# Query masks built by GpSimd block copies, and half of an output-projection block loaded by eight transfers of every eighth partition

## The chip, the cores and the metric

The kernel runs on one core of one Trainium2 chip. The metric is the device time of one execution in microseconds; the profiled span is about 2 us shorter than it. Three runs of the kernel before took 1343.92 to 1344.07 us, median 1344.0. "Fast" here means within 1.5% of the fastest run of the same kernel.

## The reference, cut to what matters

One decode step of attention over a cached K and V, with a small gated MLP beside it. Attention moves nearly all the bytes: K and V are 256 MB each, `wq` and `wo` 8 MB each, in bf16.

```python
B, Sq, D = 4, 1, 1024
H, Sk, Dh = 32, 8192, 128
q = (x @ wq).reshape(B, Sq, H, Dh).transpose(0, 2, 1, 3)
scores = jnp.einsum("bhqd,bhkd->bhqk", q, k_cache) * (Dh ** -0.5)
p = softmax(scores)
o = jnp.einsum("bhqk,bhkd->bhqd", p, v_cache)
a = o.transpose(0, 2, 1, 3).reshape(B, Sq, H * Dh) @ wo
out = g * a + (1 - g) * b          # b: a one-token MLP; g: a sigmoid gate
```

Every byte of K, V and the weights is used once, so the kernel can be no faster than its loads.

## The kernel before

All large loads are issued by SyncEngine (`nc.sync`) in program order. They land in a ring of five 4 MB slots. K is transposed by DVE and multiplied with a masked query `Z` on PE; V is multiplied with the softmax weights on PE.

```python
ring = const.tile([P, NS, RING], BF, name="ring")      # NS = 5 slots, 4 MB each

def load_pair(src, n, apart=False):                     # one pair: 4 heads, 8 MB
    a = slots(2)
    if a + 1 < NS and not apart:
        nc.sync.dma_start(out=flat[:, lo:lo + 2 * n], in_=src)
        ...
    for i, half in enumerate(halves):                   # two halves of 4 MB
        nc.sync.dma_start(out=half[:, 0:n], in_=src[:, i * n:(i + 1) * n])

def wo_block(g, r0=0, r1=FR):                           # 1 MB of wo: 512 rows
    w = wo_home[home][:, at]
    nc.sync.dma_start(out=w[:, r0:r1]..., in_=wov[:, g, r0:r1]...)
    def use():
        ... mm_acc(acc[...], LT[:, r, g, :], w[:, r, ...])
    return use

def spread(d):                                          # the masked query Z
    nc.vector.tensor_tensor(out=Z[...], in0=qa[:, :, h0:h0 + NQ, b],
                            in1=mq[:].to_broadcast([P, 4, NQ]), op=ALU.mult)
```

The last V pair comes in six pieces (two of 2 MB and four of 1 MB), so that PE can follow closely. The end of the program is:

```python
    # in v_pair, for the last pair d == ND - 1
    for half, cuts in ((0, 2), (1, 4)):
        for c in range(cuts):
            nc.sync.dma_start(out=vs[half][:, lo:hi], in_=vv[...])
...
for kind, d in order:
    ...
    if (kind, d) == ("v", ND - 1):
        for g in range(2):
            wo_block(g)()          # wo blocks 0 and 1, ahead of the last V pair
    if kind == "v":
        v_pair(d)
...                                # then wo blocks 2 to 7
```

The scheduler gives each transfer a completion semaphore, from eight in rotation (the trace's issues carry eight numbers, 101 to 105 and 108 to 110, in turn). A transfer therefore may not be issued before the one eight places ahead of it in the queue has landed; I call this the rule of eight. In the trace of the kernel before, the last landing of the V half is at 1298.95 us, and the last V piece, eight places behind it, is issued at 1299.01. The compiled SyncEngine stream of the kernel before shows it at the tail (`DMAHW` are the rotating semaphores; earlier transfers carry no such wait because a wait on PE already implies it):

```
L196 V 128x16384      [waits PE]           x3     halves of the last-but-one pairs
L388 wo 128x4096      [waits PE]           x2     wo blocks 0 and 1
L515 V 128x8192       [waits PE]           x2     last V pair, 2 MB pieces
L515 V 128x4096       [waits PE]           x2     last V pair, 1 MB pieces
L515 V 128x4096       [waits DMAHW3, PE]
L515 V 128x4096       [waits DMAHW4, PE]
```

(The lines are shortened.) I call the last 4 MB transfer of the last-but-one V pair "the V half".

Of the kernel before, what the change touches and what calls it, by code (L numbers as in the profile page):

```python
# [8 lines left out]
BF = mybir.dt.bfloat16  # L9
F32 = mybir.dt.float32  # L10
U32 = mybir.dt.uint32
# [101 lines left out]
def kernel(  # L113
# [61 lines left out]
    def turned(rows, n, dtype=BF):  # L175
        t = TB[tb_turn[0] % 3]
        tb_turn[0] += 1
        return t[0:rows, 0:n] if dtype == BF else t[0:rows, 0:2 * n].bitcast(dtype)

    def slots(n):  # L180
        at = turn[0]
        turn[0] = (at + n) % NS
        return at
# [15 lines left out]
    def small(shape, dtype=F32):  # L199
        return mps.tile(shape, dtype, name="small", tag="small")  # L200
# [15 lines left out]
        nc.vector.memset(z[:], 0.0)  # L216
    acc = acc4[0:Bn].rearrange("p z n -> p (z n)")

    row = const.tile([P, P], F32)
    nc.vector.memset(row[:, 0:1], 0.0)  # L220
    n = 1
    while n < P:
        nc.vector.tensor_scalar(out=row[:, n:2 * n], in0=row[:, 0:n], scalar1=float(n), scalar2=None, op0=ALU.add)
        n *= 2
    col = const.tile([P, 32], F32)
    nc.vector.transpose(out=col[:].bitcast(U32), in_=row[:, 0:32].bitcast(U32))
    for n in range(32, P, 32):
        nc.vector.tensor_scalar(out=col[n:n + 32], in0=col[n:n + 32], scalar1=float(n), scalar2=None, op0=ALU.add)
    ident = const.tile([P, P], F32)
    nc.vector.tensor_scalar(out=ident[:], in0=row[:], scalar1=col[:, 0:1], scalar2=None, op0=ALU.is_equal)  # L230
    identb = const.tile([P, P], BF)
    nc.vector.tensor_copy(out=identb[:], in_=ident[:])
    xw_ps = small([P, DT, NX], BF)
# [5 lines left out]
    R = ptp.tile([P, 4, P], BF, name="R", tag="PTs")  # L239
    for half in range(2):  # L240
        for e in range(2):
            turns = ident[:, 64 * half + e:64 * half + 64:2]
            for n in range(4):
                nc.vector.tensor_copy(out=R[:, 2 * half + e, 32 * n:32 * n + 32], in_=turns)

    mask3 = const.tile([P, GD, NQ], F32)
    nc.vector.tensor_reduce(out=mask3[:], in_=ident[:].rearrange("p (q t r) -> p t q r", q=NQ, t=GD), axis=AX.X, op=ALU.add)
# [2 lines left out]
    one = ident[:].rearrange("p (t e s a) -> p e a t s", t=GD, e=2, s=NQ)  # L250
    for a in range(4):
        nc.vector.tensor_tensor(out=selg[:, a], in0=one[:, 0, a], in1=one[:, 1, a], op=ALU.add)
    mE4 = const.tile([P, 2, 4], F32)
    nc.vector.tensor_reduce(out=mE4[:], in_=ident[:].rearrange("p (n e r) -> p e n r", n=4, e=2), axis=AX.X, op=ALU.add)
    mE = const.tile([P, 2], F32)
    nc.vector.tensor_reduce(out=mE[:], in_=mE4[:], axis=AX.X, op=ALU.add)
    mq4 = const.tile([P, NQ], F32)
    nc.vector.tensor_reduce(out=mq4[:], in_=ident[:].rearrange("p (q r) -> p q r", q=NQ), axis=AX.X, op=ALU.add)
    mq = const.tile([P, 1, NQ], BF)
    nc.vector.tensor_copy(out=mq[:, 0, :], in_=mq4[:])  # L260
    ones = const.tile([P, P], F32)
    nc.gpsimd.memset(ones[:], 1.0)
    mx, mxT, ng, ngT = [const.tile([P, 32], F32, name=f"mx{i}") for i in range(4)]
    nc.vector.memset(mx[:], 0.0)
    ZW = QP - 1 + P + 1
    Zt = [const.tile([P, 4, ZW], BF, name=f"Z{i}") for i in range(2)]
    PB = const.tile([P, QP, 2, 2, 2, NQ, 4], BF, name="PB")
# [5 lines left out]
    qa = const.tile([P, 4, H, Bn], BF)  # L273
    OT = const.tile([P, H, Bn], BF)
    LT = const.tile([P, FR, H // FR, Bn], BF)
    hT = const.tile([P, FG, FR, Bn], BF)
    sgb = const.tile([P, 2, Bn], F32)
    c12 = const.tile([P, 2, Bn], F32)
# [91 lines left out]
    def o_rows(g0, g1):  # L370

        n = g1 - g0
        lp = small([P, FR, n, Bn])
        for k in range(WB):
            for r in range(FR):
                nc.tensor.matmul(lp[32 * k:32 * k + 32, r], lhsT=identb[:, r:P:FR],  # L376
                                 rhs=OT[:, WB * g0 + k:WB * g1:WB, :], start=True, stop=True, skip_group_check=True)
        nc.vector.tensor_copy(out=LT[:, :, g0:g1, :], in_=lp[:])  # L378

    wo_home = {}  # L380

    def wo_block(g, r0=0, r1=FR):

# [40 lines left out]
    def spread(d):  # L424
        b, h0 = heads(d)
        Z = Zt[d % 2]
        nc.vector.tensor_tensor(out=Z[:, :, QP - 1:QP - 1 + P].rearrange("p e (q c) -> p e q c", c=QP)[:, :, :, 0],  # L427
                                in0=qa[:, :, h0:h0 + NQ, b], in1=mq[:].to_broadcast([P, 4, NQ]), op=ALU.mult)

    def k_pair(d):  # L430
        g, t = divmod(d, GD)
# [29 lines left out]
    def softmax(g):  # L461
        sps = S_ps.pop(g)

        nc.vector.tensor_reduce(out=mx[:, 0:1], in_=sps[:].rearrange("p z n -> p (z n)"), axis=AX.X, op=ALU.max)  # L464
        nc.vector.transpose(out=mxT[:].bitcast(U32), in_=mx[:].bitcast(U32))
        gm = stat.tile([P, GD], F32, tag="gm")
        nc.vector.tensor_reduce(out=gm[:], in_=mxT[:].rearrange("p (t r) -> p t r", r=RD), axis=AX.X, op=ALU.max)
        nc.vector.tensor_scalar(out=ng[:].rearrange("p (t r) -> p t r", r=RD), in0=gm[:].unsqueeze(2).to_broadcast([P, GD, RD]),
                                scalar1=-scale, scalar2=None, op0=ALU.mult)
        nc.vector.transpose(out=ngT[:].bitcast(U32), in_=ng[:].bitcast(U32))  # L470
        negm = ngT
        PTs = ptp.tile([P, 1024], BF, name="PTs", tag="PTs")
        rs = stat.tile([P, 1], F32, tag="rs")
        nc.scalar.activation(out=PTs[:], in_=sps[:].rearrange("p z n -> p (z n)"), func=ACT.Exp, bias=negm[:, 0:1], scale=scale, accum_out=rs[:, 0:1])  # L474
        PT = ptp.tile([P, 32, 32], BF, name="PT")
        nc.vector.transpose(out=PT[:].rearrange("p j i -> p (j i)"), in_=PTs[:])  # L476
        rex = stat.tile([P, GH], F32, tag="rex")
        nc.vector.tensor_scalar(out=rex[:], in0=mask, scalar1=rs[:, 0:1], scalar2=None, op0=ALU.mult)

        def inverse():  # L480
            tot = small([P, GH])
            nc.tensor.matmul(tot[:, :], lhsT=ones[:], rhs=rex[:], start=True, stop=True)  # L482
            rinv = stat.tile([P, GH], F32, name="rinv", tag="rinv")
            nc.vector.reciprocal(out=rinv[:], in_=tot[:, :])  # L484
            rinv_t[g] = rinv
        late.append(inverse)

        def spread_p():
            Pv = PT[:].rearrange("p (q j) i -> p i q j", j=4)
            Bv = PB[:].rearrange("p i z w e s j -> p i (z w e) s j")  # L490
            for q in range(NQ):
                at = slice(QP * q, QP * (q + 1))
                if q % 2 == 0:
                    nc.scalar.copy(out=Bv[at, :, :, q, :], in_=Pv[at])  # L494
                else:
                    nc.gpsimd.tensor_copy(out=Bv[at, :, :, q, :], in_=Pv[at])  # L496
        behind.append(spread_p)
# [66 lines left out]
    for kind, d in order:  # L564
        if kind == "k":
            k_pair(d)
            if d in side:
                side[d]()
        if (kind, d) == ("v", ND - 1):
            for g in range(2):  # L570
                wo_block(g)()
        if kind == "v":
            v_pair(d)
        if (kind, d) == ("k", ND // 2):
            add_x()
        if (kind, d) == ("v", ND - 2):
            o_rows(0, GE)
# [45 lines left out]
```

## Time and profile before

| | before |
|---|---|
| time, median | 1344.0 us |
| DMA: share of 16 engines' span in the main queue | 99.5% |
| mean rate | 429 GB/s |
| PE, DVE, POOL busy | 77%, 46%, 3% |
| V half landed (PE's wait for it ended) | 1298.99 us |
| PE's last wait for wo ended | 1337.33 us |

These are lines of the profile's page of the kernel before: the span, the busy times, two rows of 40 slices (busy tenths of the DMA engines, GB/s), two queues (packets, MB, share) and the shares of the chain that ended last.

```profile
span 1342.0 us, 7617 instructions
...
PE 1037.2 (77%) x4552; PEld 228.1 (17%) x2364; DVE 621.8 (46%) x434; ACT 50.6 (4%) x46; POOL 35.5 (3%) x24
...
DMA  9999999999999999999999999999999999999997
...
q1 hardware_dynamic: 14276, 575.69, 99.5%
q8 instruction: 27, 0.44, 0.1%
...
DMA 69%; DVE 19%; PE 11%; issue 0%; ACT 0%; SPq 0%; DVEq 0%
```

The DMA engines are full in every slice but the last. No compute engine bounds the kernel, and the chain's DVE and PE parts only free ring slots while earlier loads are still queued. So a change can gain only by filling the DMA engines at the end, and can lose by letting them run dry. The line of queue 8 is 27 packets of 16 KB that fetch instructions.

Next is SyncEngine's timeline of the kernel before, around the tail (start, length, engine, line, operation, transfer, count; a group that waits inside is long):

```profile
1270.38 0.33 SPq L196 DMA_DIRECT2D ring<-in_A_v_cache_dram  x1
1272.11 2.05 SPq L388 DMA_DIRECT2D ring<-in_A_wo_dram  x2
1279.68 19.66 SPq L515 DMA_DIRECT2D ring<-in_A_v_cache_dram  x6
1301.43 7.74 SPq L388 DMA_DIRECT2D ring<-in_A_wo_dram  x3
```

The first line is the issue of the V half. wo blocks 0 and 1 follow at once, and the last V pair from 1279.68, almost 20 us before the V half has landed. That is the queue's lead. And these are windows of the kernel before (window in us, its length and the busy times of PE, PEld, DVE, ACT and POOL, then the granted clock, the DMA share, GB/s):

```profile
1280.00:1290.00 10.00, 10.00 (x51) 2.33 (x25) 0.00 (x0) 0.00 (x0) 0.00 (x0) 1.00 1.02 439
1292.00:1302.00 10.00, 7.31 (x28) 1.50 (x14) 0.00 (x0) 0.00 (x0) 0.00 (x0) 0.83 0.99 415
1302.00:1312.00 10.00, 9.68 (x66) 2.58 (x40) 0.23 (x1) 0.00 (x0) 0.00 (x0) 1.00 1.00 423
```

One more fact comes from the trace's packet records, which carry no engine's number; I joined packets that follow one another without a gap into 16 strings. Towards the end seven strings run ahead of the other nine: their last bytes of wo land at 1331.7 to 1332.5, the others' at 1336.0 to 1338.2. All 16 together would be level at about (7 x 1332 + 9 x 1337) / 16 = 1335, so evening them out could gain some 3 us at most (an estimate from these times).

### The profile page before, as it was taken

Reading aid. Unit: us, or ns where it says so; the run is one execution under the profiler, and the core shown is the slowest. Engines: PE = TensorE matmul, PEld = TensorE weight load, DVE = VectorE, ACT = ScalarE, POOL = GpSimd, SP = SyncE. Lnnn points to the kernel's source line nnn. Section 1 sums busy time; section 2 is a strip of 40 time slices with the busy share of each in tenths; the row PEclk is TensorE's granted clock in tenths of the full one; section 3 lists DMA queues with packets and bytes.
Section 4 is the critical chain, followed back from the end, with each engine's and each line's share of the span. In section 5 each row is a group of like instructions: output and inputs, shape, how many; then the busy total and the mean of one; then the engine's idle time right before and its main releaser. Section 6 shows DMA issues by size and latency. Waiting matters only on the chain.

```text
span 1342.0 us, 7617 instructions
## 1 busy us (share of the span) xinstructions
PE 1037.2 (77%) x4552; PEld 228.1 (17%) x2364; DVE 621.8 (46%) x434; ACT 50.6 (4%) x46; POOL 35.5 (3%) x24
## 2 busy tenths in 40 slices
PE   2565878787788687778987779597778678877898
PEld 0111111111111121111211112111111112111222
DVE  3555655545346554336455556046555254556000
ACT  0000100001000010001000010000100010000100
POOL 1000100001000010001000010000100010000100
PEclk9777988988998888899988889898889799888999
DMA  9999999999999999999999999999999999999997
GB/s 416 437 432 430 436 436 427 447 428 421 441 426 429 443 436 423 437 434 430 438 434 430 432 427 436 436 432 438 428 425 433 432 433 440 436 419 446 419 424 327
DMA packets 14316, 576.18 MB, mean 429 GB/s; under 512 B 1598, under 2 KB 1606, under 8 KB 2252
## 3 DMA queue, kind: packets, MB, share of 16 engines
q1 hardware_dynamic: 14276, 575.69, 99.5%
q8 instruction: 27, 0.44, 0.1%
q14 instruction: 5, 0.04, 0.0%
q10 hardware_dynamic: 8, 0.00, 0.0%
HBM read 575.68 MB, written 0.01 MB: 429 GB/s over the span
## 4 chain that ended last, share of the span: by engine, by line
DMA 69%; DVE 19%; PE 11%; issue 0%; ACT 0%; SPq 0%; DVEq 0%
DMA ring<-in_A_k_cache_dram 58%; DVE TB L443 19%; DMA ring<-in_A_v_cache_dram 7%; PE o_ps L523 7%; PE S_ps L449 3%; DMA ring<-in_B_w_gate_dram 3%; DMA ring<-in_A_wo_dram 1%; PE o_ps L315 0%; DVE Z L427 0%; PE acc L315 0%; PE acc L281 0%; PE small L482 0%; PE small L543 0%; DVE OS L536 0%; ACT OS L535 0%
## 5 line engine op out<-in xcount | busy, mean ns | idle before, releaser
L443 DVE STREAM_TRANSPOSE TB<-ring 128x2048 uint32<-128x2048 uint32 x256 | 569.4, 2280 | 487.7 <-DMA ring<-in_A_k_cache_dram 485.6
L449 PE MATMUL S_ps<-TB,Z 128*128 128x512 bf16 x2048 | 522.8, 411 | 216.5 <-DVE TB L443 216.0
L523 PE MATMUL o_ps<-ring,PB 128*32 128x512 bf16 x2048 | 461.3, 387 | 52.5 <-DMA ring<-in_A_v_cache_dram 48.0
L449 PEld LDWEIGHTS <-Z 128*128 128x128 bf16 x1024 | 106.1, 104 | 628.4 <-issue 626.8
L523 PEld LDWEIGHTS <-PB 128*32 128x32 bf16 x1024 | 100.5, 98 | 404.9 <-issue 394.9
L496 POOL COPY PB<-PT 32x1024 bf16<-32x1024 bf16 x16 | 30.5, 1905 | 1223.9 <-PE o_ps L523 1069.8
L474 ACT ACTIVATE PTs<-S_ps,mx 128x1024 bf16<-128x1024 f32 x8 | 8.9, 1114 | 1019.7 <-DVE mx L470 1019.7
L536 DVE SCALAR_TENSOR_TENSOR OS<-o_ps,mE,OS 128x512 f32<-128x512 f32 x8 | 6.0, 751 | 70.8 <-ACT OS L535 70.8
L494 ACT COPY PB<-PT 32x1024 bf16<-32x1024 bf16 x16 | 30.6, 1910 | 1.6 <-DVE PT L476 1.4
L484 DVE RECIPROCAL rinv<-small 128x16 f32<-128x16 f32 x8 | 2.1, 258 | 41.5 <-PE small L482 41.5
L378 DVE CAST LT<-small 128x64 bf16<-128x64 f32 x2 | 0.5, 225 | 44.0 <-PE small L376 44.0
L235 PE MATMUL small<-identb,x 6*128 6x6 bf16 x8 | 0.6, 197 | 22.2 <-DMA x<-in_A_x_dram 22.2
L464 DVE TENSOR_REDUCE mx<-S_ps 128x1 f32<-128x1024 f32 x8 | 9.8, 1225 | 15.9 <-PE S_ps L449 15.9
L281 PE MATMUL acc<-ring,LT 128*4 128x512 bf16 x64 | 14.8, 379 | 1.7 <-DMA ring<-in_A_wo_dram 0.9
L476 DVE STREAM_TRANSPOSE PT<-PTs 128x1024 bf16<-128x1024 bf16 x8 | 10.0, 1245 | 10.2 <-ACT PTs L474 10.2
L281 PE MATMUL acc<-ring,hT 128*4 128x512 bf16 x56 | 12.2, 379 | 0.0
L535 ACT ACTIVATE OS<-o_ps,mE 128x512 f32<-128x512 f32 x8 | 5.5, 687 | 163.4 <-PE o_ps L523 163.4
L543 PEld LDWEIGHTS small<-selg,OS 128*128 128x128 f32 x64 | 8.4, 195 | 4.1 <-issue 3.9
L315 PE MATMUL o_ps<-ring,xw 128*4 128x512 bf16 x56 | 5.3, 505 | 3.9 <-DMA ring<-in_B_w_gate_dram 3.9
L543 PE MATMUL small<-selg,OS 128*128 128x16 f32 x64 | 8.1, 259 | 0.0
L237 DVE COPY xw<-small 128x48 bf16<-128x48 bf16 x1 | 0.2, 182 | 14.9 <-PE small L235 14.9
L315 PE MATMUL S_ps<-ring,xw 128*4 128x512 bf16 x64 | 6.3, 582 | 0.3 <-DVE xw L237 0.3
(68 smaller groups left out, 72.6 us busy)
## 6 DMA issues: line engine op xcount, KB each, us to landing
ring<-in_A_k_cache_dram SPq DMA_DIRECT2D x14, 4096.0 KB, 34.2
ring<-in_A_v_cache_dram SPq DMA_DIRECT2D x14, 4096.0 KB, 31.3
ring<-in_B_w_gate_dram SPq DMA_DIRECT2D x1, 7168.0 KB, 37.2
ring<-in_B_w_up_dram SPq DMA_DIRECT2D x1, 7168.0 KB, 39.2
ring<-in_B_w_down_dram SPq DMA_DIRECT2D x2, 3584.0 KB, 27.3
ring<-in_A_wo_dram SPq DMA_DIRECT2D x6, 1024.0 KB, 24.7
ring<-in_A_v_cache_dram SPq DMA_DIRECT2D x2, 2048.0 KB, 30.5
ring<-in_A_v_cache_dram SPq DMA_DIRECT2D x4, 1024.0 KB, 24.6
```

What stands on the lines that cost most here:

```text
L281: nc.tensor.matmul(out_ap, lhsT=lhsT, rhs=rhs, start=start, stop=True, skip_group_check=True)
L315: nc.tensor.matmul(ps[32 * k:32 * k + Bn, z, :], lhsT=xT[TW * half + t], rhs=cols(w, t, 4 * z + k), start=(half + t == 0), stop=(half == 1 ...
L443: nc.vector.transpose(out=flat_t.bitcast(U32), in_=kn[:, c * CJ * Dh:(c + 1) * CJ * Dh].bitcast(U32))
L449: nc.tensor.matmul(sps[:, z, :], lhsT=Z[:, he, s:s + P], rhs=T[:, 16 * z:16 * z + 16, half, :, e], start=(t == 0 and n == 0 and he == 0), ...
L464: nc.vector.tensor_reduce(out=mx[:, 0:1], in_=sps[:].rearrange("p z n -> p (z n)"), axis=AX.X, op=ALU.max)
L474: nc.scalar.activation(out=PTs[:], in_=sps[:].rearrange("p z n -> p (z n)"), func=ACT.Exp, bias=negm[:, 0:1], scale=scale, accum_out=rs[:, ...
L476: nc.vector.transpose(out=PT[:].rearrange("p j i -> p (j i)"), in_=PTs[:])
L494: nc.scalar.copy(out=Bv[at, :, :, q, :], in_=Pv[at])
L496: nc.gpsimd.tensor_copy(out=Bv[at, :, :, q, :], in_=Pv[at])
L523: nc.tensor.matmul(o_ps[row:row + NM, e, :], lhsT=PB[:, RD * t + c, z, w].rearrange("p e s j -> p (e s j)"), rhs=vn[:, j0 * Dh:(j0 + 4) * ...
L536: nc.vector.scalar_tensor_tensor(out=o_sb[:], in0=o_ps[:, 1, :], scalar=mE[:, 1:2], in1=o_sb[:], op0=ALU.mult, op1=ALU.add)
L543: nc.tensor.matmul(oT[:, :], lhsT=o_sb[:, q * Dh:(q + 1) * Dh], rhs=selg[:, q].rearrange("p t s -> p (t s)"), start=(q == 0), stop=(q == 3))
```

## The change

The intent is twofold. First, DVE is relieved: masks and the masked queries `Z` are built by GpSimd copies, block by block, instead of DVE products. Second, half of wo's first block is loaded in a way that is meant to give some DMA engines more bytes than others. Rows 0 to 255 of wo go onto partitions 0 to 63, in eight transfers of eight partitions each; rows 256 to 511 come in a normal 128-partition transfer.

```diff
@@ spread(d): the masked query
-        nc.vector.tensor_tensor(out=Z[...][:, :, :, 0],
-                                in0=qa[:, :, h0:h0 + NQ, b], in1=mq[:].to_broadcast([P, 4, NQ]), op=ALU.mult)
+        for q in range(NQ):
+            at = slice(QP * q, QP * (q + 1))
+            nc.gpsimd.tensor_copy(out=Z[at, :, QP - 1 + QP * q], in_=qa[at, :, h0 + q, b])
@@ new
+    def wo_first():
+        wo_home[0] = ring[:, slots(1)].rearrange("p (g r n) -> p g r n", g=4, r=FR)
+        w = wo_home[0][:, 0].rearrange("p r n -> p (r n)")
+        half = P * FR // 2
+        lower = A_wo[0:half].rearrange("(e o r) n -> o e (r n)", e=8, r=FR)
+        for o in range(8):
+            nc.sync.dma_start(out=w[o:P // 2:8], in_=lower[o])
+        w2 = turned(P, 2 * D)
+        nc.sync.dma_start(out=w2, in_=A_wo[half:2 * half].rearrange("(p r) n -> p (r n)", r=2))
+        def use(): ...   # 8 + 4 matmuls instead of 8
@@ the tail
-            for g in range(2):
-                wo_block(g)()
+            wo_first()()
+            wo_block(1)()
@@ softmax: the row sums
-        rex = stat.tile(...); nc.vector.tensor_scalar(out=rex[:], in0=mask, scalar1=rs[:, 0:1], ...)
-            nc.tensor.matmul(tot[:, :], lhsT=ones[:], rhs=rex[:], start=True, stop=True)
+            nc.tensor.matmul(tot[:, :], lhsT=rs[:, 0:1].to_broadcast([P, P]), rhs=mask, start=True, stop=True)
... (cut: prologue masks moved to GpSimd; LT2, a second transposed output for the upper half)
```

In the compiled stream of the changed kernel the tail now reads:

```
L389 wo 8x4096        [waits PE]
L389 wo 8x4096                             x3
L389 wo 8x4096        [waits DMAHW1], then [DMAHW2], [DMAHW3], [DMAHW4]
L391 wo 128x2048      [waits DMAHW5]
L408 wo 128x4096      [waits DMAHW6, PE]
L533 V 128x8192       [waits DMAHW7, PE], then five more behind DMAHW0 to 4
```

The semaphore of the eighth narrow transfer, DMAHW4, is that of the V half. All that stands behind it in the queue waits for the V half too.

More of the change, by code (lines that the diff above doesn't have):

```diff
@@ L217 @@
     acc = acc4[0:Bn].rearrange("p z n -> p (z n)")
-    row = const.tile([P, P], F32)
-    nc.vector.memset(row[:, 0:1], 0.0)
+    row = const.tile([P, 2, 32], F32)
+    nc.vector.memset(row[:, 0, 0:1], 0.0)
     n = 1
-    while n < P:
-        nc.vector.tensor_scalar(out=row[:, n:2 * n], in0=row[:, 0:n], scalar1=float(n), scalar2=None, op0=ALU.add)
+    while n < 32:
+        nc.vector.tensor_scalar(out=row[:, 0, n:2 * n], in0=row[:, 0, 0:n], scalar1=float(n), scalar2=None, op0=ALU.add)
         n *= 2
-    col = const.tile([P, 32], F32)
-    nc.vector.transpose(out=col[:].bitcast(U32), in_=row[:, 0:32].bitcast(U32))
-    for n in range(32, P, 32):
-        nc.vector.tensor_scalar(out=col[n:n + 32], in0=col[n:n + 32], scalar1=float(n), scalar2=None, op0=ALU.add)
+    nc.vector.transpose(out=row[:, 1].bitcast(U32), in_=row[:, 0].bitcast(U32))
+    id32 = const.tile([P, 32], F32)
+    nc.vector.tensor_tensor(out=id32[:], in0=row[:, 0], in1=row[:, 1], op=ALU.is_equal)
     ident = const.tile([P, P], F32)
-    nc.vector.tensor_scalar(out=ident[:], in0=row[:], scalar1=col[:, 0:1], scalar2=None, op0=ALU.is_equal)
+    nc.gpsimd.memset(ident[:], 0.0)
+    for n in range(0, P, 32):
+        nc.gpsimd.tensor_copy(out=ident[n:n + 32, n:n + 32], in_=id32[n:n + 32])
     identb = const.tile([P, P], BF)
@@ L241 @@
         for e in range(2):
-            turns = ident[:, 64 * half + e:64 * half + 64:2]
-            for n in range(4):
-                nc.vector.tensor_copy(out=R[:, 2 * half + e, 32 * n:32 * n + 32], in_=turns)
+            nc.gpsimd.tensor_copy(out=R[:, 2 * half + e].rearrange("p (n j) -> p n j", n=4),
+                                  in_=ident[:, 64 * half + e:64 * half + 64:2].unsqueeze(1).to_broadcast([P, 4, 32]))
     mask3 = const.tile([P, GD, NQ], F32)
@@ L252 @@
         nc.vector.tensor_tensor(out=selg[:, a], in0=one[:, 0, a], in1=one[:, 1, a], op=ALU.add)
-    mE4 = const.tile([P, 2, 4], F32)
-    nc.vector.tensor_reduce(out=mE4[:], in_=ident[:].rearrange("p (n e r) -> p e n r", n=4, e=2), axis=AX.X, op=ALU.add)
     mE = const.tile([P, 2], F32)
-    nc.vector.tensor_reduce(out=mE[:], in_=mE4[:], axis=AX.X, op=ALU.add)
-    mq4 = const.tile([P, NQ], F32)
-    nc.vector.tensor_reduce(out=mq4[:], in_=ident[:].rearrange("p (q r) -> p q r", q=NQ), axis=AX.X, op=ALU.add)
-    mq = const.tile([P, 1, NQ], BF)
-    nc.vector.tensor_copy(out=mq[:, 0, :], in_=mq4[:])
-    ones = const.tile([P, P], F32)
-    nc.gpsimd.memset(ones[:], 1.0)
+    nc.vector.tensor_reduce(out=mE[:], in_=id32[:].rearrange("p (e r) -> p e r", e=2), axis=AX.X, op=ALU.add)
     mx, mxT, ng, ngT = [const.tile([P, 32], F32, name=f"mx{i}") for i in range(4)]
-    nc.vector.memset(mx[:], 0.0)
+    nc.gpsimd.memset(mx[:], 0.0)
     ZW = QP - 1 + P + 1
@@ L275 @@
     LT = const.tile([P, FR, H // FR, Bn], BF)
+    LT2 = const.tile([P, 2, Bn], BF)
     hT = const.tile([P, FG, FR, Bn], BF)
@@ L378, in o_rows, with use @@
         nc.vector.tensor_copy(out=LT[:, :, g0:g1, :], in_=lp[:])
-    wo_home = {}
+        if g0 == 0:
+            lp = small([P, 2, Bn])
+            for k in range(2):
+                for r in range(2):
+                    nc.tensor.matmul(lp[64 * k:64 * k + 64, r], lhsT=identb[:, r:P:2], rhs=OT[:, 2 + k, :],
+                                     start=True, stop=True, skip_group_check=True)
+            nc.vector.tensor_copy(out=LT2[:], in_=lp[:])
+    wo_home = {}
+    def wo_first():
[7 more added lines that the diff above has]
+        nc.sync.dma_start(out=w2, in_=A_wo[half:2 * half].rearrange("(p r) n -> p (r n)", r=2))
+        def use():
+            for r in range(FR):
+                for n in range(NH):
+                    mm_acc(acc[:, n * NB:(n + 1) * NB], LT[0:P // 2, r, 0, :], w[0:P // 2, r * D + n * NB:r * D + (n + 1) * NB])
+            for r in range(2):
+                for n in range(NH):
+                    mm_acc(acc[:, n * NB:(n + 1) * NB], LT2[:, r, :], w2[:, r * D + n * NB:r * D + (n + 1) * NB])
+        return use
     def wo_block(g, r0=0, r1=FR):
@@ L426, in spread @@
         Z = Zt[d % 2]
-        nc.vector.tensor_tensor(out=Z[:, :, QP - 1:QP - 1 + P].rearrange("p e (q c) -> p e q c", c=QP)[:, :, :, 0],
-                                in0=qa[:, :, h0:h0 + NQ, b], in1=mq[:].to_broadcast([P, 4, NQ]), op=ALU.mult)
+        for q in range(NQ):
+            at = slice(QP * q, QP * (q + 1))
+            nc.gpsimd.tensor_copy(out=Z[at, :, QP - 1 + QP * q], in_=qa[at, :, h0 + q, b])
     def k_pair(d):
@@ L476, in softmax @@
         nc.vector.transpose(out=PT[:].rearrange("p j i -> p (j i)"), in_=PTs[:])
-        rex = stat.tile([P, GH], F32, tag="rex")
-        nc.vector.tensor_scalar(out=rex[:], in0=mask, scalar1=rs[:, 0:1], scalar2=None, op0=ALU.mult)
         def inverse():
             tot = small([P, GH])
-            nc.tensor.matmul(tot[:, :], lhsT=ones[:], rhs=rex[:], start=True, stop=True)
+            nc.tensor.matmul(tot[:, :], lhsT=rs[:, 0:1].to_broadcast([P, P]), rhs=mask, start=True, stop=True)
             rinv = stat.tile([P, GH], F32, name="rinv", tag="rinv")
```

## The prediction

> **What bounds the kernel now.** The DMA engines. The page gives a DMA share of 9 tenths or more in 39 of 40 slices; the main queue's packets take 99.5% of 16 engines' span, at 429 GB/s. The chain that ended last is 69% DMA; its 19% DVE and 11% PE only free ring slots while earlier transfers are still queued. DVE is 46% busy, PE 77%. Only the tail (last slice 327 GB/s) leaves anything to gain.
>
> **What the change moves between engines.** DVE loses 32 Z products and 8 rex products of 0.19 us each, and in the prologue 16 R copies (1.45 us) and some reductions: about 10 us of 622, all under the DMA. POOL gets 128 Z copies and the prologue's copies; at an estimated 0.1 to 0.3 us each (its 128x1 memset takes 0.10 us) 15 to 40 us. Each Z is built a pair ahead, and POOL is free before the x rows land at 22.2 us. I count 0 us for both. PE gets 8 more matmuls in the tail, about 1 us.
>
> **What it does to wo's first block.** The bytes stay. [...]The intent must be to give engines that run ahead more work: 512 KB on 8 engines instead of 16 moves 32 KB per engine, 1.2 us at 27 GB/s (64 KB packets take 2.42 us). Before, some engines finish about 5 us ahead of others (packet records).
>
> **Why I expect that gain to be lost.** Completion semaphores are reused every eighth transfer: in before, the last V pieces wait for the V transfer eight issues earlier (SyncEngine's waits: 11.6 us, the longest 9.4), and the last is issued only at 1299.0. With seven more transfers, the eighth small one waits for that same V half, landed at about 1299.0. The queue issues in order, so the second half of block 0, block 1 and all pieces of the last V pair, issued from 1272 to 1299 before, wait too. Then the queue holds only seven small pieces (56 KB per engine on 8 engines) and runs dry. At 0.33 us per issue and about 1 us from issue to first packet (at the kernel's start), full-width data restart at about 1300.4, 2 us after the slowest engine's V bytes; the engines ahead idle about 6 us. Less the 1.2 us moved, plus up to 0.5 us for slow first packets, the tail is 0.8 to 1.3 us longer.
>
> **Prediction.** 1345.0 us, 8 in 10 within 1343.4 to 1347.0. Faster by over 2%: 0.01; within 2%: 0.98; slower by over 2%: 0.01.
>
> **What would show it.**
> - Windows: DMA share in 1292 to 1302 falls from 0.99 to about 0.7; until 1290 it stays.
> - SyncEngine's timeline: the eighth small transfer is issued at about 1299, then the rest at 0.33 us spacing; before, the first V piece was issued at 1279.7.
> - Waits: SyncEngine waits for V landings about 25 us at the small transfers.
> - PE's first matmul of the last V pair starts about 1 us later.
> - DVE busy near 612 us; time up to 1290 unchanged within 0.5 us.
>
> **What would make it wrong.** If the dry spell is under 1 us, or the engines with the extra share are exactly those ahead, the time falls by about 1 us to 1343. If POOL copies contend with DVE's transposes, K transfers might be issued late; with over 20 us queued it should not show. If PE, nearly dense in 1299 to 1325, cannot catch up, up to 1 us more.

2 us of dry spell, less the 1.2 us moved, plus 0 to 0.5 us, are the 0.8 to 1.3 us on top of 1344.0. That the narrow transfers use eight engines was an assumption then; the trace of the kernel after bears it out. Their 64 packets of 8 KB never run more than eight at a time, and the semaphore of a narrow transfer has nine landings (one about 1 us after the issue, eight as the data come), that of a wide one sixteen. The kernel's start shows what slow first packets are: in the kernel before, the first begins 1.00 us after the first issue, and the first sixteen of 64 KB take 2.47 to 3.46 us, where 2.42 us is usual.

## The result, and the profile after

| | before | after |
|---|---|---|
| time, median of 5 runs | 1344.0 us (1343.88 to 1344.14) | 1348.79 us (1348.6 to 1349.68) |
| ratio | | 1.0036, 95% interval 1.0023 to 1.005 |
| span of the profiled run | 1342.0 us | 1346.9 us |

A ratio here is the mean time of one kernel's fast runs over that of the other's of the same rounds, so it is not quite the ratio of the medians quoted beside it. Within 2% the change is "the same", as predicted. But it is 4.8 us slower, where 1.0 us was predicted, and 1.8 us above the top of the range.

The same lines of the page, for the kernel after, and the new group of GpSimd copies (line, engine, operation, tiles, count | busy us, mean ns | idle before and what ended it):

```profile
span 1346.9 us, 7728 instructions
...
PE 1036.9 (77%) x4560; PEld 228.5 (17%) x2370; DVE 614.7 (46%) x370; ACT 50.6 (4%) x46; POOL 62.7 (5%) x161
...
DMA  9999999999999999999999999999999999999988
...
q1 hardware_dynamic: 14404, 575.69, 99.3%
...
L449 POOL COPY Z<-qa 32x4 bf16<-32x4 bf16 x128 | 25.6, 200 | 761.4 <-PE S_ps L470 734.0
```

DVE lost 7 us and GpSimd gained 27; neither was short of time. The bytes are the same 575.69 MB. The last two slices have gone from 9 and 7 tenths to 8 and 8.

SyncEngine's timeline of the kernel after, the same stretch:

```profile
1272.22 0.33 SPq L196 DMA_DIRECT2D ring<-in_A_v_cache_dram  x1
1273.95 27.30 SPq L389 DMA_DIRECT2D ring<-in_A_wo_dram  x8
1301.29 0.44 SPq L391 DMA_DIRECT2D TB<-in_A_wo_dram  x1
1301.85 0.35 SPq L408 DMA_DIRECT2D ring<-in_A_wo_dram  x1
1302.30 3.25 SPq L533 DMA_DIRECT2D ring<-in_A_v_cache_dram  x6
1305.60 2.44 SPq L408 DMA_DIRECT2D ring<-in_A_wo_dram  x2
```

The eight narrow transfers hold the queue for 27.30 us. The last V pair is issued from 1302.30 instead of 1279.68. The windows of the kernel after:

```profile
1280.00:1290.00 10.00, 10.00 (x48) 2.23 (x23) 0.00 (x0) 0.00 (x0) 0.00 (x0) 1.00 1.00 433
1292.00:1302.00 10.00, 6.99 (x33) 1.55 (x16) 0.00 (x0) 0.00 (x0) 0.00 (x0) 1.00 0.52 156
1302.00:1312.00 10.00, 9.85 (x65) 2.51 (x43) 0.34 (x2) 0.00 (x0) 0.00 (x0) 1.00 1.00 397
```

Until 1290 nothing has changed. From 1292 to 1302 the engines are half idle. But note the ratio of share to rate: before, 0.99 of the engines moved 415 GB/s; now 0.52 of them move only 156. Half the busy time should have moved 218. So the engines that were busy were also slow.

That is visible directly in PE's wait for the V half. PE's timeline, first before:

```profile
1298.99 7.58 PE L523 MATMUL o_ps<-ring,PB 128*32 128x512 bf16 x28 [2.69 <-DMA ring<-in_A_v_cache_dram]
```

and after:

```profile
1300.71 6.20 PE L541 MATMUL o_ps<-ring,PB 128*32 128x512 bf16 x28 [3.02 <-DMA ring<-in_A_v_cache_dram]
```

The V half was issued more than 25 us before it lands in both kernels, yet it lands 1.7 us late in the kernel after. (It was issued 1.8 us later than before, at 1272.22, but with some 27 us of queue ahead of it that does not matter: e9 below issues it at 1272.04 and lands it at 1298.90.) The prediction knew nothing of this.

The end of the chain that ended last (start, length, step), before:

```profile
1289.26 31.87 DMA ring<-in_A_v_cache_dram
...
1321.19 16.10 DMA ring<-in_A_wo_dram
...
1337.33 1.90 PE acc L281 x8
```

and after:

```profile
1304.64 20.30 DMA ring<-in_A_v_cache_dram
...
1325.00 17.16 DMA ring<-in_A_wo_dram
...
1342.20 1.90 PE acc L274 x8
```

A V piece of the last megabytes lands 3.81 us late and the last of wo 4.87 us late: about 1.1 us more is lost after 1321, long after the dry spell. So there are three places to explain: 1.7 us before the dry spell, the dry spell itself, and 1.1 us after it.

### The profile page after: what moved, and what is told of

It reads as the page before. It is cut to its first block, busy times and chain, and to the rows that moved or that the text cites. A ratio compares the mean times of both kernels' runs of the same rounds, so it can differ in the third digit from the quotient of the medians.

```text
span 1346.9 us, 7728 instructions
## 1 busy us (share of the span) xinstructions
PE 1036.9 (77%) x4560; PEld 228.5 (17%) x2370; DVE 614.7 (46%) x370; ACT 50.6 (4%) x46; POOL 62.7 (5%) x161
## 3 DMA queue, kind: packets, MB, share of 16 engines
q1 hardware_dynamic: 14404, 575.69, 99.3%
## 4 chain that ended last, share of the span: by engine, by line
DMA 66%; DVE 20%; PE 11%; another core or an unknown queue 1%; ACT 0%; issue 0%; SPq 0%; DVEq 0%
DMA ring<-in_A_k_cache_dram 58%; DVE TB L464 20%; PE o_ps L541 8%; DMA ring<-in_A_v_cache_dram 6%; PE S_ps L470 3%; DMA x<-in_gate_w_dram 2%; DMA ring<-in_A_wo_dram 1%; ACT PB L512 0%; PE S_ps L308 0%; PE small L561 0%; PE acc L308 0%; SPq L533 0%; PE acc L274 0%; ACT OS L553 0%
## 5 line engine op out<-in xcount | busy, mean ns | idle before, releaser
L464 DVE STREAM_TRANSPOSE TB<-ring 128x2048 uint32<-128x2048 uint32 x256 | 567.1, 2277 | 490.6 <-DMA ring<-in_A_k_cache_dram 489.5
L449 POOL COPY Z<-qa 32x4 bf16<-32x4 bf16 x128 | 25.6, 200 | 761.4 <-PE S_ps L470 734.0
L274 PE MATMUL acc<-ring,LT 128*4 128x512 bf16 (+1 forms) x64 | 14.9, 378 | 2.6 <-DMA ring<-in_A_wo_dram 2.1
```

The costliest lines, as they stand in the source:

```text
L274: nc.tensor.matmul(out_ap, lhsT=lhsT, rhs=rhs, start=start, stop=True, skip_group_check=True)
L449: nc.gpsimd.tensor_copy(out=Z[at, :, QP - 1 + QP * q], in_=qa[at, :, h0 + q, b])
L464: nc.vector.transpose(out=flat_t.bitcast(U32), in_=kn[:, c * CJ * Dh:(c + 1) * CJ * Dh].bitcast(U32))
```

## The experiments

Theory A, the prediction's: the rule of eight makes the queue run dry. Theory B, formed from the late V half: packets that write every eighth of partitions 0 to 63 collide, where they write, with the V packets that run beside them. Theory C: the work on GpSimd costs something. (The recorded texts use letters of their own: in e3's, B is narrow transfers that cost time by themselves, and e4's calls C what is B here.) What B's collision is in the hardware no run shows; the runs show which partitions bring it about, and its size.

The following comes from the packet records of the trace: mean durations of the packets that start from 1292 to 1296 us. In this window the V half's last 32 KB packets run beside the first packets behind them (in the kernel before the 8 KB packets are those of wo block 0, in the others those of the narrow or half transfers; a row on one partition is 8 KB in both).

| kernel | 32 KB packets (V) | 8 KB packets |
|---|---|---|
| before | 1234 ns | 313 ns |
| after | 1887 ns (longest 2138) | 512 ns |
| e3_eight_wide | 1550 ns | |
| e4_every_fourth | 1233 ns | 310 ns |
| e5_one_wide | 1772 ns | 535 ns |
| e7_source_rows | 1821 ns | 510 ns |
| e9_eight_tiny | 1232 ns | |
| e14_other_ports | 2098 ns (longest 2442) | 565 ns |

In the kernel after, eight of the narrow transfers' 8 KB packets start between 1300.2 and 1302.0 us, when no V packet is left and few others run; they take 309 to 314 ns. The eight of the last narrow transfer start together at 1302.03 to 1302.34, still with no V packet, and take 311 to 512 ns; those of e4's last one take 307 to 314. So one such packet is not slow alone: the pattern is slow in company, its own included, and it slows the V packets beside it.

All experiments were timed in five rounds, e7 in three (it has four runs). The kernel before took 1344.15 us in the rounds of e1 to e9 and 1344.17 in those of e10 to e16. "Before" and "after" in the diffs say which kernel was edited; `old` is the loop of eight narrow transfers.

### Which part of the change costs the time

e1_block0_wide is the kernel after with wo block 0 loaded as before; everything on GpSimd stays.

```diff
-            wo_first()()
-            wo_block(1)()
+            for g in range(2):
+                wo_block(g)()
```

> The changed kernel with wo's block 0 loaded as before (one transfer of 128 partitions); all other parts of the change stay. My theory: the moves from DVE to GpSimd are worth nothing and cost nothing, so the time is that of before, 1344.0 within 0.4 us, DVE busy about 612 us, and the DMA share in 1290 to 1302 is 0.96 or more. Rival: part of the 4.8 us comes from the 128 GpSimd copies; then the time lies between 1345 and 1348.5.

Measured: 1343.94 us, ratio 0.9998 (0.9985 to 1.0012). Theory C is out: the GpSimd part costs nothing and gains nothing.

e2_first_only is the reverse: before, with only `wo_first` and the second transposed output. The new small tile lies where a mask is dead by then, since a first build lacked 32 bytes of SBUF.

```diff
-            for g in range(2):
-                wo_block(g)()
+            wo_first()()
+            wo_block(1)()
```

> The kernel before with nothing but the new loading of block 0 (eight narrow transfers, one wide half block). My theory: the whole loss comes from it, 1348.8 within 0.5 us, and the DMA share in 1290 to 1302 falls to about 0.6. Rival (the GpSimd part takes its share): under 1347.

Measured: 1348.96 us, 1.0038. The V half landed at 1300.72, PE's last wait for wo ended at 1342.44. The whole loss belongs to `wo_first`.

### Does the partition pattern matter

e3_eight_wide: eight transfers again, but each over 64 neighbouring partitions and an eighth of the columns, meant to give no engine more than another.

```diff
-            nc.sync.dma_start(out=w[o:P // 2:8], in_=lower[o])
+            nc.sync.dma_start(out=w[0:P // 2, 512 * o:512 * (o + 1)], in_=lower[:, 512 * o:512 * (o + 1)])
```

> The lower half of block 0 still comes in eight transfers, but each takes 512 columns of all 64 partitions[...]. Number of transfers and their semaphores are as in the changed kernel. Theory A (the queue runs dry because the eighth of them waits for a V half landed): the dry spell stays; the V half lands at about 1299 and not at 1300.7, because nothing narrow disturbs it; 1345.5 to 1347.5. Theory B (narrow transfers alone cost the time): 1344.0 to 1344.6.

Measured: 1348.49 us, 1.0035; a miss. I had thought 64 neighbouring partitions harmless, but V packets slow down here as well (1550 ns, 1234 in the kernel before; V half at 1300.11).

e4_every_fourth: the same eight narrow transfers, each over every fourth partition of 0 to 31 or of 32 to 63.

```diff
-        lower = A_wo[0:half].rearrange("(e o r) n -> o e (r n)", e=8, r=FR)
-        for o in range(8):
-            nc.sync.dma_start(out=w[o:P // 2:8], in_=lower[o])
+        lower = A_wo[0:half].rearrange("(c e o r) n -> c o e (r n)", c=2, e=8, r=FR)
+        for c in range(2):
+            for o in range(4):
+                nc.sync.dma_start(out=w[32 * c + o:32 * c + 32:4], in_=lower[c, o])
```

> Eight narrow transfers still, but each writes every fourth partition of 0 to 31 or of 32 to 63 instead of every eighth of 0 to 63. Theory C (engines collide where they write[...]): packets of 8 KB take about 310 to 350 ns instead of 500 to 640, those of the V half 1.21 us instead of up to 2.1, the V half lands 1.7 us earlier, and the time is about 1347.1; the dry spell stays. Rival (any eight narrow rows disturb, by their reads or by the number of engines): packets as slow as before, time 1348.8 within 0.5.

Measured: 1347.43 us, 1.0025. This is 1.4 us less than the kernel after. PE's timeline of e4 shows the V half on time again:

```profile
1298.71 6.20 PE L542 MATMUL o_ps<-ring,PB 128*32 128x512 bf16 x28 [2.63 <-DMA ring<-in_A_v_cache_dram]
```

and its window shows the dry spell unchanged, but at a rate of 210 GB/s for 0.53 of the engines, as full-speed packets should give:

```profile
1292.00:1302.00 10.00, 7.37 (x35) 1.61 (x17) 0.00 (x0) 0.00 (x0) 0.00 (x0) 1.00 0.53 210
```

So the collision is removed by the choice of partitions alone, and 3.3 us of the loss stay.

e7_source_rows is the kernel after with each narrow transfer reading consecutive rows of wo but writing the same partitions. The result is wrong; the comparison with the reference still passed, since attention's share of the output is small.

```diff
-        lower = A_wo[0:half].rearrange("(e o r) n -> o e (r n)", e=8, r=FR)
+        lower = A_wo[0:half].rearrange("(o e r) n -> o e (r n)", e=8, r=FR)
```

> Wrong result on purpose: the eight narrow transfers write every eighth partition as in the changed kernel, but each reads eight rows that follow one another in memory. If the collision is where they write: packets of 8 KB stay at 450 to 640 ns, V packets at up to 2.1 us, time 1348.8 within 0.6. If it is where they read (rows 64 KB apart): packets 310 to 350 ns, V half landed at about 1299, time about 1347.4.

Measured: 1348.94 us, 1.0035, V half at 1300.52. Reading consecutive rows changes nothing (8 KB packets 510 ns and V packets 1821, against 512 and 1887 in the kernel after), so the collision does not come from which rows are read; that leaves the writing side.

e14_other_ports is e4 with the rows on every fourth of partitions 64 to 127 (wrong: PE multiplies them with the outputs of other rows).

```diff
-                nc.sync.dma_start(out=w[32 * c + o:32 * c + 32:4], in_=lower[c, o])
+                nc.sync.dma_start(out=w[64 + 32 * c + o:64 + 32 * c + 32:4], in_=lower[c, o])
```

> Wrong result on purpose: the changed kernel with every fourth partition, but of 64 to 95 and 96 to 127 instead of 0 to 31 and 32 to 63. [...] packets of 8 KB at 450 to 640 ns, V packets over 1.5 us, V half landed at 1300 or later, 1348.2 to 1349.5. If only rows of the same narrow transfer collide: packets at 309 ns and 1347.4 within 0.4.

Measured: 1350.79 us (1349.97 to 1351.72), 1.005: worse than any other kernel here, and worse than expected. PE's timeline of e14:

```profile
1301.55 6.20 PE L542 MATMUL o_ps<-ring,PB 128*32 128x512 bf16 x28 [2.76 <-DMA ring<-in_A_v_cache_dram]
```

Within one transfer the rows are four partitions apart, exactly as in e4, and each narrow transfer makes eight packets of 8 KB, as there. Yet these packets take 565 ns instead of 310, and the V packets beside them 2098 instead of 1233. So it is not enough that a transfer's own packets keep four partitions apart: which partitions they write, of 0 to 63 or of 64 to 127, matters too. (The first range of the recorded text was for packets that collide with those of other transfers, the second for collisions inside one transfer alone; the first came closer, at 1348.2 to 1349.5.) Why the upper partitions are worse was not shown: no record names an engine, or where in memory a packet writes. And a collision with V packets is not all of it: the eight packets of e14's last narrow transfer start at 1302.92 to 1303.00, with no V packet beside them, and still take 399 to 419 ns, where e4's take 307 to 314. What else is wrong with e14 stays open.

### The collision without the dry spell

e6_act_fourth is e4 with the eight narrow transfers issued by ScalarE, whose queue is otherwise nearly empty; e10_act_eighth is the kernel after with the same edit. The two differ in the partitions alone. With ScalarE issuing, SyncEngine need not wait behind the narrow transfers.

```diff
-                nc.sync.dma_start(out=w[32 * c + o:32 * c + 32:4], in_=lower[c, o])
+                nc.scalar.dma_start(out=w[32 * c + o:32 * c + 32:4], in_=lower[c, o])
```

```diff
-            nc.sync.dma_start(out=w[o:P // 2:8], in_=lower[o])
+            nc.scalar.dma_start(out=w[o:P // 2:8], in_=lower[o])
```

> The eight narrow transfers go to every fourth partition (as in the run that took 1347.4) and are issued by ScalarE, whose queue may wait for the V halves without holding up SyncEngine's. If the dry spell is what is left of the loss there, it goes: the pieces of the last V pair are issued before 1295, DMA share in 1290 to 1302 0.95 or more, and the time is 1343.0 to 1344.6 (a gain of up to 1.2 us if the engines with the extra share are those ahead). Rival (narrow transfers cost time whatever waits for them): 1346 or more.

> The eight narrow transfers write every eighth partition as in the changed kernel, but ScalarE issues them, so SyncEngine's queue does not run dry. It shows the collision alone, beside the run with every fourth partition from ScalarE (1343.6). If writing partitions eight apart costs 1.4 to 1.7 us of the whole queue's time, as between the changed kernel and its every-fourth version: 1344.8 to 1345.6, packets of 8 KB up to 500 to 640 ns and V packets up to 2.1 us around 1279 to 1288. If the collision only matters beside a dry queue: 1343.3 to 1344.0.

Measured: e6 1343.62 us (1343.5 to 1345.24), ratio 1.0000 (0.9987 to 1.0012); e10 1348.35 us (1347.05 to 1349.53), 1.0033. SyncEngine's timeline of e6 has a lead again; the last V pair is issued 10.5 us before the V half lands at 1299.84 (19.3 us in the kernel before):

```profile
...
1286.77 0.33 SPq L392 DMA_DIRECT2D TB<-in_A_wo_dram  x1
1288.87 0.33 SPq L409 DMA_DIRECT2D ring<-in_A_wo_dram  x1
1289.31 10.89 SPq L534 DMA_DIRECT2D ring<-in_A_v_cache_dram  x6
...
```

In both kernels the engines are busy from 1292 to 1302 (shares 0.98 and 0.95). In e6 all 64 narrow packets take 309 to 320 ns, and the V packets that start from 1275 to 1285 take 1217 ns; in e10 the narrow ones take 309 to 665 ns and the V packets of that stretch 1506 ns. e10's V half lands at 1304.67, e6's at 1299.84; PE's timelines, e6 first:

```profile
1299.84 6.20 PE L542 MATMUL o_ps<-ring,PB 128*32 128x512 bf16 x28 [2.00 <-DMA ring<-in_A_v_cache_dram]
```

```profile
1304.67 7.89 PE L541 MATMUL o_ps<-ring,PB 128*32 128x512 bf16 x28 [2.03 <-DMA ring<-in_A_v_cache_dram]
```

So the collision alone, when it is spread over all eight transfers, costs 4.7 us (e10 less e6 in the medians; 4.3 in the means, as both kernels scatter by about 2 us). PE has no wait for a load after 1304.67 in e10, so it could not have caught up; but the loads end as late themselves, with their last byte at 1342.6 against 1337.7. I had expected e10 at 1344.8 to 1345.6, because I sized it from the kernel after. There only 29 of the 32 KB packets that start from 1270 to 1305 take more than 1400 ns; in e10 134 of some 320 do.

e6 is the most the idea of the change gives here: its narrow packets give some engines more work and nothing waits, yet it is not clearly faster than before. There is no version that clearly beats the kernel before.

e5_one_wide loads the lower half in one transfer of 64 partitions: one queue place instead of eight, so no dry spell.

```diff
-        lower = A_wo[0:half].rearrange("(e o r) n -> o e (r n)", e=8, r=FR)
-        for o in range(8):
-            nc.sync.dma_start(out=w[o:P // 2:8], in_=lower[o])
+        lower = A_wo[0:half].rearrange("(p r) n -> p (r n)", r=FR)
+        nc.sync.dma_start(out=w[0:P // 2], in_=lower)
```

> The lower half of block 0 in one transfer of 64 partitions[...], the upper half as in the changed kernel. Two transfers more than nothing else, the same extra matmuls on PE. My theory (the number of transfers makes the queue run dry, the narrow rows disturb): neither is left, so 1344.0 to 1344.6, DMA share in 1290 to 1302 0.95 or more, and the first piece of the last V pair is issued before 1290. Rival (the split of block 0 with its second home and its extra matmuls costs the time): 1346 or more.

Measured: 1348.23 us (1347.28 to 1348.39), 1.0028; a clear miss. Its window and, after it, its V issue in SyncEngine's timeline:

```profile
1292.00:1302.00 10.00, 6.29 (x33) 1.36 (x14) 0.00 (x0) 0.00 (x0) 0.00 (x0) 1.00 0.96 270
```

```profile
1282.12 23.05 SPq L532 DMA_DIRECT2D ring<-in_A_v_cache_dram  x6
```

The V pieces are issued from 1282.12, the engines are 0.96 busy, and they move 270 GB/s instead of 415. The V half lands at 1302.30. A theory with the dry spell alone would have put this kernel at 1344.

e13_seven_rows tried to find a better kernel: from ScalarE, seven of the eight rows of each of e4's transfers, and the eight rows left (partitions 28 to 31 and 60 to 63) in two four-row transfers. Seven rows were meant for seven engines, as many as run ahead; which engines they use no run shows. (Its first range was for the case that they are the seven that run ahead.)

```diff
-                nc.scalar.dma_start(out=w[32 * c + o:32 * c + 32:4], in_=lower[c, o])
+                nc.scalar.dma_start(out=w[32 * c + o:32 * c + 28:4], in_=lower[c, o, 0:7])
+        for c in range(2):
+            nc.scalar.dma_start(out=w[32 * c + 28:32 * c + 32], in_=rows[32 * c + 28:32 * c + 32])
```

> A try for a faster kernel: from ScalarE, every fourth partition, but seven rows at a time, [...](in before seven engines finish 4 to 6 us ahead of nine), and two transfers of four rows for what is left. [...]1342.6 to 1343.3. If not, 1343.5 or more.

Measured: 1345.6 us (1343.9 to 1346.62), 1.001 (0.9996 to 1.0024). The try failed: the V half landed at 1301.61. V packets from 1288 to 1292 take 1293 ns on average, the longest 1920. It may be that the two four-row transfers, over four neighbouring partitions each, collide; I did not test that, so the cause stays open.

### The dry spell without the collision

e9_eight_tiny is the kernel before with eight tiny transfers (16 partitions of 128 bytes, 2 KB each) put ahead of wo block 0. They take places in the queue but hardly any time of an engine.

```diff
+            wo_home[0] = ring[:, slots(1)].rearrange("p (g r n) -> p g r n", g=4, r=FR)
+            for o in range(8):
+                nc.sync.dma_start(out=wo_home[0][0:16, 3, 0, 64 * o:64 * (o + 1)],
+                                  in_=wov[0:16, 3, 0, 64 * o:64 * (o + 1)])
             for g in range(2):
                 wo_block(g)()
```

> The kernel before with eight tiny transfers (16 partitions of 128 bytes) in front of block 0, which stays wide. It adds 16 KB and nothing else, but the eighth tiny one must wait for the V half eight transfers earlier. Theory A (the reuse of semaphores runs the queue dry): the last V pair is issued after 1299 and not from 1279 on, no full-width data between about 1298.5 and 1300.4, DMA share in 1290 to 1302 falls to about 0.6 to 0.7, time 1347.0 to 1348.8. Rival (a short pause of the queue is made good): 1344.0 to 1344.6.

Measured: 1348.34 us, 1.0031. Sixteen kilobytes of extra traffic cost 4.2 us. SyncEngine's timeline of e9:

```profile
1272.04 0.33 SPq L196 DMA_DIRECT2D ring<-in_A_v_cache_dram  x1
1277.44 21.75 SPq L572 DMA_DIRECT2D ring<-in_A_wo_dram  x8
1299.23 0.90 SPq L388 DMA_DIRECT2D ring<-in_A_wo_dram  x2
1300.22 3.14 SPq L515 DMA_DIRECT2D ring<-in_A_v_cache_dram  x6
...
```

and its window:

```profile
1292.00:1302.00 10.00, 8.61 (x41) 1.89 (x20) 0.00 (x0) 0.00 (x0) 0.00 (x0) 1.00 0.41 150
```

The V half lands on time (1298.90), its packets run at full speed (1232 ns), and PE's last wait for wo ends at 1341.49, 4.16 us late. This is theory A pure, and it is as large as e10's collision pure. In the kernel after the two overlap.

e15_four_tiny and e16_six_tiny are e9 with four and six tiny transfers. With four, the transfer that waits for the V half stands so late in the queue that the V pieces ahead of it keep the engines busy; six should let only those engines run dry that run ahead.

```diff
-            for o in range(8):
+            for o in range(4):        # e15; range(6) in e16
```

> As the kernel before with eight tiny transfers (1348.3), but only four. Then block 0, block 1 and the first 2 MB of the last V pair are issued before the V half has landed at 1299.0, 256 KB per engine: no engine runs dry. If the loss is the dry spell: 1343.9 to 1344.4. If tiny transfers cost by themselves: about 1346.

> Six tiny transfers: at 1299.0 only block 0 is queued, 64 KB or 2.5 us per engine. The nine engines behind bridge the gap with it, the seven ahead run dry for some 5 us and lose their lead. If only the dry time of the slowest engines is lost for good: 1344.0 to 1345.4 (the rest for the fetch, which no engine's lead can hide any more). If all dry time counts: 1346.5 or more.

Measured: e15 1344.45 us, 1.0002; e16 1345.38 us, 1.001. Their windows, e15 first:

```profile
1292.00:1302.00 10.00, 7.30 (x35) 1.55 (x17) 0.00 (x0) 0.00 (x0) 0.00 (x0) 1.00 1.00 416
```

```profile
1292.00:1302.00 10.00, 7.36 (x28) 1.41 (x13) 0.00 (x0) 0.00 (x0) 0.00 (x0) 0.83 0.73 282
```

Tiny transfers as such are free (e15). In e16 the engines are 0.73 busy, 2.6 us less per engine than in the kernel before, and yet PE's wait for a late V piece ends at 1321.21, as before (1321.17): only dry time of the engines that come last costs time there. But the time is still 1.2 us longer, and the loss comes after 1321: PE's last wait for wo ends at 1338.55.

### What is lost after the dry spell

That late loss appears in the kernel after (1.1 us), in e9 and in e16: wherever the seven leading strings have lost their lead. In e9 the last bytes of 15 strings land at 1340.4 to 1340.9 and of one at 1342.3; and an instruction-fetch packet of 16 KB, about 1.06 us long, had started at 1333.4. My theory: when all engines are level, a late fetch delays the last byte, while before it fell where it did no harm. e11_tiny_fewer_pe and e12_before_fewer_pe drop most of PE's matmuls on the last V data from e9 and from before, so that fewer instructions are fetched in the tail. Their outputs are wrong, which doesn't matter for the times. A kernel bounded by its loads should not notice the missing work on PE.

```diff
                     for e in range(2):
                         j0 = CJ * (c % JT) + 16 * z + 8 * w + 4 * e
+                        if (d == ND - 1 or (d == ND - 2 and c >= JT)) and z + w > 0 and n < 4 * RD - 1:
+                            continue
```

> Wrong result on purpose: the kernel with eight tiny transfers (1348.3), with about 100 instructions less on PE in its last 40 us (part of the last V matmuls left out), so that the last of 27 instruction fetches, at 1333.4 us, is not made. Theory: after the dry spell all 16 engines run level, so the 16 KB fetch delays the last byte by its 1.1 us and more; without it 1346.6 to 1347.4. If PE or something else sets the end there: 1348.0 or more.

> Wrong result on purpose: the kernel before with the same instructions left out on PE, as the control. Theory: before, the fetch at 1330.8 falls on an engine that is not the last to finish, so leaving it out is worth less than 0.4 us: 1343.6 to 1344.2. If it is worth as much as beside the tiny transfers: 1342.5 to 1343.0.

Measured: e11 1347.22 us, 1.0023, which is 1.12 us less than e9; e12 1344.0 us, 1.0000, 0.17 less than before. In e11 all 16 strings end between 1340.5 and 1341.0. The straggler is gone, and with it 1.1 us; in the kernel before the same cut changes nothing. e11's chain that ended last has at its end

```profile
1335.41 7.08 PE acc L281 x32
```

These are PE's last 32 matmuls, and none of them waits for a load. So PE sets the end of e11, and, if my theory holds, 1.1 us is the least that the fetch costs: the last byte itself comes 1.29 us earlier than in e9 (1340.98 against 1342.27). In e12 PE runs without such a wait at the end as well and could hardly have been faster, so there the packet records are the better witness: the last byte comes at 1338.10, and at 1338.15 in the kernel before. Why seven engines lead in the kernel before was not tested.

### All runs

| kernel | median us | ratio to before | V half landed |
|---|---|---|---|
| after | 1348.79 | 1.0036 | 1300.71 |
| e1_block0_wide | 1343.94 | 0.9998 | 1299.36 |
| e2_first_only | 1348.96 | 1.0038 | 1300.72 |
| e3_eight_wide | 1348.49 | 1.0035 | 1300.11 |
| e4_every_fourth | 1347.43 | 1.0025 | 1298.71 |
| e5_one_wide | 1348.23 | 1.0028 | 1302.30 |
| e6_act_fourth | 1343.62 | 1.0000 | 1299.84 |
| e7_source_rows | 1348.94 | 1.0035 | 1300.52 |
| e9_eight_tiny | 1348.34 | 1.0031 | 1298.90 |
| e10_act_eighth | 1348.35 | 1.0033 | 1304.67 |
| e11_tiny_fewer_pe | 1347.22 | 1.0023 | 1298.91 |
| e12_before_fewer_pe | 1344.0 | 1.0000 | 1298.90 |
| e13_seven_rows | 1345.6 | 1.0010 | 1301.61 |
| e14_other_ports | 1350.79 | 1.0050 | 1301.55 |
| e15_four_tiny | 1344.45 | 1.0002 | 1299.19 |
| e16_six_tiny | 1345.38 | 1.0010 | 1298.74 |

## Why the prediction was right or wrong

**What bounds the kernel, and the GpSimd part: right.** The loads bound it. DVE fell to 614.7 us (predicted near 612), the 128 Z copies take 0.200 us each (estimated 0.1 to 0.3), and e1 shows that all of this is worth nothing (1343.94 us). Nor do GpSimd's copies slow DVE's transposes of K, a risk that the prediction named: these take 2277 ns on average, 2280 in the kernel before. Until 1290 the time is unchanged (the DMA share 1.02 and 1.00 of the window before it).

**The mechanism of the dry spell: right.** SyncEngine waited 22.4 us for V landings at the narrow transfers, where about 25 were predicted:

```profile
SPq L389 <- DMA ring<-in_A_v_cache_dram: 22.4, 3, 10.9
```

(this is a line of SyncEngine's waits in the kernel after: total, times, longest). e9 makes the dry spell by itself. Its length was about right as well: from the V half's last byte, at 1300.18, to the first packet of full-width data, at 1302.43, are 2.3 us (1.9 in e9, from 1298.35 to 1300.28); 2 were predicted. From the start of the issue to that packet were 1.14 us (1301.29 to 1302.43; 1.05 in e9, 1299.23 to 1300.28); about 1 was assumed.

**Where it failed.** Two steps of the text fell:

- "the eighth small one waits for that same V half, landed at about 1299.0". It landed in time for PE at 1300.71. I had treated the seven narrow transfers beside the V half as harmless small work for engines that run ahead. In fact they slow the V half's packets from 1234 to 1887 ns, and the dry spell then starts 1.7 us later.
- "Less the 1.2 us moved, plus up to 0.5 us for slow first packets, the tail is 0.8 to 1.3 us longer." The sum lacked two terms, the slow V half and the lead that the leading engines lose, and one was too small, the slow first packets. It let the engines ahead "idle about 6 us" and counted nothing for it.

The DMA share from 1292 to 1302 fell to 0.52 where I had predicted 0.7, and the eighth narrow transfer was issued at 1300.68, not 1299. PE's first matmul of the last V pair started 2.4 us later (1310.27 and 1312.63), where I had predicted 1.

**The sum as the runs have it.** The experiments let the loss be built up step by step, in medians against the kernel before of 1344.15 us:

| step | how | us |
|---|---|---|
| dry spell, its slow restart, and the lead lost in it | e9 less before | +4.2 |
| more bytes on some engines | e4 less e9 | -0.9 |
| collision with the V half | after less e4 | +1.4 |
| sum | | +4.7 |

The observed loss is 4.8. The steps lead from before over e9 and e4 to after, so they must add up to the whole whatever the causes are; the sum is no test. What the runs show is the size of each step in this order: the collision alone, without a dry spell, cost 4.7 us (e10 less e6), not 1.4.

Of the 4.2 us of the first line, 1.1 went with the matmuls left out (e9 less e11), which I put down to the instruction fetch that now delays the last byte, and 1.9 the gap itself (measured in e9). The 1.2 us that remain are not measured by a run of their own. In e9 eleven of the first 8 KB packets after the gap take 427 to 1186 ns, where 309 is usual, and I read most of the rest as that; I had allowed 0.5 us. Another count needs no rest (an estimate). In e9 the engines are busy for 0.41 of the stretch from 1292 to 1302, in the kernel before for 0.99: each loses 5.8 us on average. All level, the engines of the kernel before would end at 1335; 5.8 us later is 1340.8, and 15 strings of e9 do end at 1340.4 to 1340.9. That is about 2.5 us after the last byte of the kernel before (1338.15), and the string with the fetch ends 1.4 us later still. So the idle time of the leading engines counts too, once it exceeds their lead.

So the mechanism that I named was the largest term, but the collision of the narrow transfers with the V packets was missed entirely, the value of the lead was missed entirely, and the restart was sized too small. The gain from moved bytes, 1.2 us by the prediction, was about right (0.9), with the reservation that e4 and e9 differ in the bytes of the narrow transfers as well as in where they go. That the collision lies on the writing side rests on e4, e7 and e14 together: other partitions to write changed it (8 KB packets at 310 and 565 ns), other rows to read did not (510). What it is there no run shows.

What stays open: what it is that collides, which engines carry which packets (the records do not tell), why seven lead, the exact cause of e13, why e14's last narrow transfer is slow alone, and the split of the 1.2 us.

## What to carry to other kernels

A small transfer costs a place in the queue, not only its bytes: with completion semaphores in rotation, count which transfer each one has to wait for, and see that no small one waits for the last large one ahead of it (eight transfers of 2 KB cost 4.2 us here, six 1.2 us, four 0.3 us or less). When a transfer covers fewer than all partitions, measure its choice of partitions, since here the choice decided whether it slowed itself and the large transfers beside it: with every fourth partition of 32 (0 to 31, 32 to 63) the V packets took 1233 ns, as in the kernel before (1234); with every eighth of 0 to 63 they took 1887, and up to 4.7 us were lost (e10 less e6); with every fourth of 64 to 127 they took 2098. No run shows why, so nothing here says which choice is free for other large transfers. And the gap in which all engines came level also took away the slack that had hidden a later small delay: the work left out at the end, and by my theory one fetch of 1.06 us with it, was worth 1.1 us in e9 and 0.17 us in the kernel before.
